# The same operations of a convolution and an attention layer in another stored order

## The chip, the core and the metric

The kernel runs on one core of a Trainium2 chip. The core has a matrix engine (TensorE, in the profile PE, its weight loads PEld), a vector engine (DVE), a scalar engine (ACT), a general engine (POOL) and a queue engine (SP), each with its own instruction stream, and 16 DMA engines. The metric is the time of one execution in device microseconds, compared by the median of several runs.

## The reference

Two independent layers share the output, 640 columns each, over 2048 tokens, in bfloat16. Layer A is a gated long convolution, layer B attention in 4 segments of 512 tokens with a memory carried from segment to segment (32 heads of 20).

```
# A: short filter of 4 taps, gate, long convolution over the sequence by FFT, gate
k_shift = sum over t of k_pad[:, t:t+S] * shift_k[:, 3-t]
kv = k_shift * v
y = irfft(rfft(kv, 2S) * rfft(ssm_k, 2S))[:S] + kv * ssm_D
a = q * y
# B: for each segment s
p = softmax(qs @ ks.T * scale + mask)      # mask: key may not come after the query
a_dot = p @ vs
a_mem = (phi(qs) @ M) / (phi(qs) @ z + 1e-6)
o = g * a_mem + (1 - g) * a_dot            # g = sigmoid(beta) per head
M = M + phi(ks).T @ vs;  z = z + sum(phi(ks))
b = o @ wo
out = concatenate([a, b])
```

## The kernel before

The kernel is not written in the order in which it runs. A recorder (class Recorder, line 105) takes down every operation with its operands and what it depends on; a group of matmuls that accumulate together is one operation. There are 1501 operations and 470 groups of PSUM banks (8 banks of 512 columns). A stored list, ORDER (line 775), then gives the sequence in which they are issued, and a second one, BASE (line 797), the first bank of each group. Both are packed numbers; unpack (line 804) makes lists of them, and Recorder.issue (line 244) goes through them:

```
for i in order:
    o = self.ops[i]
    assert all(p in seen for p in o.pred)
    for eng, method, args, kw, grp in o.calls:
        f = getattr(getattr(self.real, eng), method)
        f(*[fix(a) for a in args], ...)
```

So all instructions carry one line in the profile, L253, and are told apart by tiles. Each engine runs its own operations in the order of the list; a wait at the head of its stream holds all that stands behind it. That includes DMAs: nearly all loads and all transposes by DMA are issued from SP, one after the other, the stores to the output from POOL.

The operations have names (their keys), used below:

Layer A runs over 5 blocks of 128 channels (conv, line 378). "sk" loads the long filter (and copies it), "lk", "lv", "lq" load k, v, q; "ks" is the short filter on PE, gated into tile vt by DVE; "FK" and "FX" are the forward transforms of filter and signal on PE (Wf, 256 columns a matmul), evicted by ACT into the one tile F; "BK" and "BX" are the butterflies on DVE, "P1" to "P3" the product, "YB" the butterflies back; "I" is the inverse transform on PE, gated by DVE into outa, "O" with a block's number its store.

Layer B runs over 8 units u, two halves of 16 heads for each segment (project, line 569; attend, line 637). "P u t" projects k or q for 128 tokens (5 matmuls of 320 columns, evicted by ACT into the one tile KQ), "V u t" the values; "KT" transposes KQ by DMA into KQT, of which there are two, one for each half; "phi", "PT" and "mem" serve the memory. "bound u" finds a bound of each row's scores on DVE (tile kam, from KQT) and PE, ACT evicts it (bT), and the four copies "rows u" put it into KQT as an extra row. Then come the scores: "S u g A", "D" and "J" fill two pairs of PSUM banks with 32-row matmuls (A below the diagonal, D on it, J joined for two head groups), and two exponentials on ACT write one of 7 tiles ET, 128 x 1024 each. "O u g q" multiplies them with the values (matmuls of 21 columns), "N u g" normalises on DVE into o_s. "oT" transposes o_s, "W" projects it, "OB" stores (project_out, line 729). For the last segment "oT" and "W" come in three parts, "first", "mid" and the rest, and the accumulation in PSUM goes through all three.

In the old list, ahead of what the change moves, PE has for unit 4 the fills "S 4 3 A", "S 4 3 D" and "S 4 2 D" in a row with nothing between, the last of them the last reader of KQT before unit 6 overwrites it. At the end PE has both column halves of "W 3 3 first", then "O 7 3", then the middle parts of "oT 3".

Of the kernel before, what the change touches and what calls it, by code (L numbers as in the profile page):

```python
# [774 lines left out]
ORDER = r"""
c-jrrgLW7S5Cy>9yLan0we8flZKt+v+qP{dwQbwBZR@>nm~$qrq!5vG5?#_uJc%qRC6#25jFMUcC9_PI88TBKCNU8~;z~pb5S6b&2``x>jpUL@5?>NX42dbRB(@}!#FA7JNiwM<NhG<XMHO+0h1`-&
(jkjfm8=p?vP%LaL=MR*$&mtCkQLeRT`Ef=e3QgThB%TEv5^XCP)G_(5h*GKq@a|N(vnB=N(m_`#iY38ll)Rf%1U}<KxU*yAmShilA^Z6M;$3AHKmqRlOU-saS;z0kqI@Vu{4o}(pnlxC@C)$rGnI#
Hqu<`$~<W)4Wy~mlk8|Ap(Tv8k^&fjoM<LJkpsEV3%PL<c~B5-rJW2!d+8vZWE_U0qm0K0OhZ0&k<OAAQ6#F2L{}+<Q5cJ<7=*#-jXvlm6EF-DF&(2Z2K_Mwvt_R2M_H6dIdqr8=pnN(1HEJjW@0G5
qc7^A9~!`I5<=Nz{6G;D!v}oC94U%V_>2e^(duKCL^m_qLM%d0`H3I$3;z(#!dnzuEK6ke|Af7zugt*$%*8@kB&ARqWw2D1$$VKL^AT3mqFNsrD#N6oR6s>6MkTD2Xf_Y9^%BEY$p%?28)b!Tl7?uE
{!$zz@l!U-02wHQqy}oD7HXpoN+71Kl}4zHDu`uOQ4LKHgu1AXb+Sd8Vz@Lzh^&zjvRZ<rIliDR+MzvKpcVe2CB9*Z43@3Z0Y@dQZIkWN5u>CvcF0aSD7z%G?Unr!PTF9kbjBe$ES<1Vy5P8U#cnwu  # L780
-OwF><d+<gV{%eX$ZzR^J#t#A>sOqTB{(Bz<(x#a0Q-$UI4>9El7zM}wg&6a(pp(3>uj+tuB}BE>uPbVkzJI=*3Oz+Z|h@&t%3ElB$m`#STAd618lrZka!l~5?gyqXvwUDtwu*1XrpC}jFSX5S*Az`
f^iUsa9OU%dL**3vH?`rNixWW*kNphsOkz#lT}!Wzw%Fp8nm`9#WI-I)8sbHuF7&um20vCJFyG9F;Vs)j7HF~8c}b^b-5`~HJXOfy$G$hB%I!s=o(&QXk?9~QM8T*XkFch$8rFhuo+vh72EJcj$l6;
>QOY(V>pGTdKzc39p`WyZLPmGvpaGgXK(@CteM`Ei?}O~<RtpqLpgyAmeG3HWn95kTtj#3XRR%hwXy4HVwZ3O59GeY)LUq32{o3cwRD!=5^Hizp^3D<p0NhnSd-{&G|`vxN?yxOeIs!+jV9ID8du|K
GQESlNMR{$q&<~q@?2g>DtnA4c!)=MinN+iQ)y}q)O0%BnrnK^Y+3Cd?&AUC>j=wY88oB*vrL*<v+5`tZDVb`J+&<Q%!FfXoTauj)=~qlmA26D_QN`AC;e*QEHrCsHp^}~ET`qQT-ILmS$^xFd-RRH
wU3tDYG^Ipss*f|6|th0#|qg;`6OTDt-O<BmQ4#=cKsl2wVig>E}B4#TMjK@IrTN(;In+P+?q@CXjko~`Lv|9);9XtUfFB=W4raQm9=tK-ty}+yq6bviMM!%=Xh+Ttc;bmC-w>xtb$dxDpu91S&&sU
r}3RtvYJNLvf5V1s#{&FVfE~#g<^fnt6@0NK3G^zvI6?s!n2@8WCRw{!usCYuq~h43!7roY^qgZRerI#Hs6|Zo+-g*Y{&L&&K8_ywYW>?*iWm?aGY*+INN60UM-^g^p{0qHO{cbw!|h|ab0T5te6(n
07heEF1HmHg>@OkMqFSG`5q;-q%N}38kGyJjF#2zy53gVY74dy+hCh)jjgouT29y6M%!$MwTJf99d<;kXeq6#TdbG%)}6M?`sh{*((Sg*_Ui%d#%g*{cUw(1<{{l@`|W@ow7z=CqI0P3wLNy!y6~8_
W&<|iaa(7H?Su`}&K#^m^rQ{cL3+ea*+?CwUD=(dtrO2$3=Y>G9HFCijP}>DI!*`ZHjT&ljLDX4#ql~pdvT&xXAMr$$vQ>ru|E5-1NSolPwR2*&Fy+ZPwFYn&NEs;r|D6xs8e;i&d?k@t2x<EXX-4S
t#fsb9@F!7!Om+(UeL>WMX%X)J7?$gqFu7fcE#rDRl8w*8JqnWhjDp>H`$Z@dDCuLWxdAh9KetK#DpBgL`=;4+@TNnlmod`Z`&QaYxnHFC1Fxl(qz1-cNvTKcuAk|8B;MelQShB*h70{?-|H6Ov`jk
!4F)fulSmInUDFIff<>J3p6vcFg@pMR=(g%F4D!iL>KCJUe#+_fCX8I*Y$?p(!wmtBFx1+ys7uKxaVeBmScH7)(R}f;(VyzSb`P#KufX|pXeif%o6^NPxY?e(`<aMFSIo8=rb+prTn$N(L#QQh5ajQ  # L790
`E%Cx;Vi>S9Kj#_$&sw$w^-F*>MQ-lKfKM~9Lw<>$K|?0SLsR}%)cDPe>AWBf5k)iR!4I=#o_PtgO1@^U8mDHoijL-Ls{N8=xv?F6<o<-Ea$WNUO(!3oxn+4t)CgJA^J%x_(Xo;WKLlNujEr%**EGY
{j5v4S-0q1F6BJV=K?O|GS1;5e$lV`P1oou26HtFctH<g4PV2xe8aa~$Fg42H*ym<a|^d}F}HC8ziVh;&oExyf9MYG<SrKTu)dpn7|tX3cJAd*-N$-f+RJ!-Kfv%F*$=XzH}YTVAfk9wZ|X%nq6c^#
uj`S#sMAAvV}Hm;tmZ-Pp2U-S6F<VE{H+x|nn(8-9@AraGmq`byt%jX*51-nd7!8ExE{~r`yWl<Ej*zo_mm#T6Zv0F>?e7O$9aP3J%wlT%$~)wdN$AQIXr`B^faE<5AiU&`acz<^PHZ`b9)}o>-jvt
clS2l&5zL#3ZVhC^>#keNBL;K%qzS|#c5t*d+*@k5FQcG(K~r(@8UhYr$<CoL_>7MKyUBkeZ8Oe_W?f8m-`qGgO%RP2l-$h;zNCy5BC*5!pHhJAMa;4!6*7zUgad8?B}@5&oeBhcqB~q=|00}`YfOA
0hr@+eV$+T>psor`vPC+i+r)K@m0Rg*ZUG*>#O~gAN9z%;lUo_SNyau^@D!MkNFng>YIGCpYtd<?-#huxBCX)=!gBdpYS7o#xM9uzv;L9s_*cNzSH;kHNWj={gUtXeZI?g`+h&*{{i6J>gE
"""
# [76 lines left out]
```

## Time and profile before

| | us |
|---|---|
| median of 3 runs | 290.04 (289.86 to 291.36) |
| the profiled execution | 290.99 |
| its span, first to last instruction | 289.2 |
| PE, DVE, ACT busy | 258.5, 262.0, 254.0 |
| mean granted clock of TensorE | 0.987 |

The profiled execution took 290.99 us, of which 289.2 lie between its first and last instruction. The views used below are the page, the busy time of each engine by stretch, the waits (the engine that waited, and for whom: total, times, longest), the chain of waits that ended last, and the timeline: start and length in us, engine, operation, output tile <- input tiles, shape, count, and in brackets the idle time before it with what ended it. SPq is a DMA issue on SP; its length is that of the issue, not of the transfer.

### The profile page before, as it was taken

What the parts mean: (1) busy time and instruction counts of PE and PEld (TensorE: products, weight loads), DVE (VectorE), ACT (ScalarE), POOL (GpSimd) and SP (SyncE); (2) the same over time, 40 slices, a digit from 0 to 9 for tenths busy, and PEclk for the clock granted to TensorE, in tenths of its full rate; (3) what the DMA queues carried; (4) which work ended last, traced back from release to release, by engine and by line L of the source; (5) the groups of instructions that cost most, each with busy time, mean ns of one, the idle gap of its engine ahead of it and who ended that gap; (6) DMA issues with size and microseconds to landing.
All of it is one profiled execution on the core that took longest, in us unless ns stands there. A gap on an engine that the chain in (4) does not pass through costs nothing. (4 is left out here: it accounts for less than half of the span.)

```text
span 289.2 us, 9883 instructions
## 1 busy us (share of the span) xinstructions
PE 258.5 (89%) x4226; PEld 195.3 (68%) x4226; DVE 262.0 (91%) x398; ACT 254.0 (88%) x391; POOL 42.5 (15%) x71
## 2 busy tenths in 40 slices
PE   0999998789989899999989999998799977888895
PEld 0788756668667678777656888656586755656673
DVE  0569999999999999999999999999999999989554
ACT  1694899899998978999999999999979999989972
POOL 8300000001005000403100310022001220001620
PEclk9999999999999989999999999999799999999999
DMA  6999889899943779916696149952492029921252
GB/s 190 383 243 178 217 160 174 207 215 164 223 118 85 165 99 204 205 61 120 166 167 144 43 59 174 191 133 71 88 156 57 24 55 141 207 26 48 58 123 91
DMA packets 113500, 40.71 MB, mean 141 GB/s; under 512 B 105696, under 2 KB 111376, under 8 KB 113328
## 3 DMA queue, kind: packets, MB, share of 16 engines
q1 hardware_dynamic: 108624, 34.07, 61.8%
q0 software_dynamic: 2064, 4.76, 5.5%
q10 hardware_dynamic: 2768, 1.24, 1.8%
q8 instruction: 33, 0.54, 0.8%
q14 instruction: 11, 0.09, 0.1%
HBM read 14.11 MB, written 5.24 MB: 67 GB/s over the span
## 5 line engine op out<-in xcount | busy, mean ns | idle before, releaser
L253 ACT ACTIVATE ET<-ps 128x1024 bf16<-128x1024 f32 x160 | 155.9, 1064 | 6.7 <-PE ps L253 6.4
L253 PEld LDWEIGHTS <-xT 128*128 128x128 bf16 x640 | 60.5, 99 | 32.2 <-issue 10.8
L253 PE MATMUL ps<-wqkv,xT 128*128 128x320 bf16 x480 | 75.5, 303 | 3.6 <-ACT ET L253 1.9
L253 ACT CAST F<-ps 128x512 bf16<-128x512 f32 x80 | 43.0, 614 | 4.2 <-DVE F L253 1.6
L253 POOL DMA_DIRECT2D out_dram<-outa x32 | 22.2, 815 | 165.1 <-DVE outa L253 141.1
L253 PEld LDWEIGHTS <-ET 128*128 128x128 bf16 x1296 | 40.3, 97 | 4.1 <-issue 2.2
L253 PE MATMUL ps<-Va,ET 128*128 128x21 bf16 x1280 | 41.2, 172 | 0.1
L253 PE MATMUL ps<-KQT 32*128 32x128 bf16 (+2 forms) x896 | 34.5, 242 | 2.0 <-ACT ET L253 1.0
L253 PEld LDWEIGHTS <-Wf 128*128 128x128 bf16 x320 | 29.9, 98 | 6.5 <-issue 2.4
L253 ACT CAST KQ<-ps 128x320 bf16<-128x320 f32 x64 | 27.5, 454 | 3.7 <-PE ps L253 3.1
L253 PE MATMUL ps<-wo,xT 128*128 128x320 bf16 x160 | 25.2, 299 | 1.1 <-ACT ET L253 0.6
L253 PEld LDWEIGHTS <-KQT 32*128 32x128 bf16 x896 | 16.5, 94 | 12.0 <-issue 10.8
L253 PE MATMUL ps<-skd,kr 128*128 128x128 bf16 (+3 forms) x140 | 20.9, 301 | 1.1 <-ACT ET L253 1.0
L253 PE MATMUL ps<-Y,Wi 128*128 128x256 bf16 x160 | 20.3, 273 | 1.7 <-ACT ET L253 1.0
L253 PE MATMUL ps<-vt,Wf 128*128 128x256 bf16 x160 | 20.1, 272 | 1.8 <-DVE vt L253 1.4
L253 PE MATMUL ps<-kT,Wf 128*128 128x256 bf16 x160 | 21.2, 276 | 0.0
L253 PEld LDWEIGHTS <-kr 128*128 128x128 bf16 x140 | 17.3, 146 | 5.5 <-issue 2.7
L253 DVE TENSOR_TENSOR o<-ps,rr 128x640 bf16<-128x640 f32 x24 | 19.7, 823 | 0.7
L253 PE MATMUL ps<-mright,mleft 32*128 32x128 bf16 x512 | 14.4, 219 | 6.5 <-ACT ET L253 3.4
L253 PE MATMUL ps<-Mbd,PqT 128*128 128x84 bf16 x96 | 18.2, 202 | 1.9 <-ACT ET L253 0.9
L253 DVE TENSOR_TENSOR Y<-Y,pq 128x2048 bf16<-128x2048 bf16 (+1 forms) x20 | 18.6, 949 | 0.1
L253 DVE TENSOR_TENSOR pq<-Xh,Kh 128x2048 bf16<-128x2048 bf16 x15 | 18.3, 1223 | 0.4
(77 smaller groups left out, 356.4 us busy)
## 6 DMA issues: line engine op xcount, KB each, us to landing
vt<-in_A_v_dram SPq DMA_DIRECT2D x10, 256.0 KB
pq<-in_A_q_dram SPq DMA_DIRECT2D x10, 256.0 KB
out_dram<-outa POOLq DMA_DIRECT2D x32, 64.0 KB, 2.5
out_dram<-outb POOLq DMA_DIRECT2D x12, 160.0 KB, 3.1
ET<-in_A_ssm_k_dram SPq DMA_DIRECT2D x3, 512.0 KB
Wf<-c_wf SPq DMA_DIRECT2D x2, 512.0 KB
...
```

The costliest lines, as they stand in the source:

```text
L253: f(*[fix(a) for a in args], **{k: fix(v) for k, v in kw.items()})
```

## The change

The lists ORDER and BASE are replaced, nothing else. By its own description the new list comes from a search that charged every stretch in which PE streams few columns. All 1501 operations are the same, on the same engines, with the same shapes. On PE 309 of 502 operations stand in another place, on DVE 265 of 398, on ACT 285 of 395, on SP 90 of 139, on POOL 54 of 67; none moves by more than 25 places in its engine's order. From about the 357th operation of ACT and the 413th of PE on, up to PE's 466th, the two lists agree but for which half of a pair comes first.

```diff
 ORDER = r"""
-c-jrrgLW7S5Cy>9yLan0we8flZKt+v+qP{dwQbwBZR@>nm~$qrq!5vG5?#_uJc%qRC6#25jFMUcC9_PI88TBKCNU8~;z~pb5S6b&2``x>jpUL@5?>NX42dbRB(@}!#FA7JNiwM<NhG<XMHO+0h1`-&
...
+c-jrsgJKv85Cp)x+r7F?Z9BDX+o^5awr$%<ZQHhO+j?()VxmeMNh{GsB%P#}6p~U>Nd}21sU?<Vlt>aNnPs}nlo=8rF(jryVp;^rB_=BI<f~9BNqEU2aV3)^kTjB55?FkxA}$FfktCBOQdMGEZpkUx
...
 BASE = r"""
-c-l=<0TRO?2#W~v{~r%R?7UtrB7_jE0XXn_vsQ;8%HCM?M0v7&S^L>p#c!S+o}I@7Ms@D4r;$)Gp@^V8p00sf7crc9MwDS=s?|&yHF(x6yH0Ws?gry9BUw2WW3-N#Z}ONm#jmTSSOx2Vh{m<m06m~(
...
+c-l=<0S?3<2rCHq{~u3FCCkOB2&DzC;8*|xhJC(yR-F@$b)Qr4^`7qi?s+0y=VvL#<@w#a6SGnF!Hu&&kIkDg62u2Hn(iP9n8lbih`5D+StRdEXs(!~h8$jvUb0~_^f?)C#7b#szW2q%)0rE;RpbG(
...
```

Three places, as the instructions stand. First PE in unit 4, before the change, where the fill "S 4 3 D" ends (KQT) and "S 4 2 D" begins (mleft):

```order
5517 L253 LDWEIGHTS KQT_81
5518 L253 MATMUL ps<-KQT_81 128x128
5519 L253 LDWEIGHTS KQT_81
5520 L253 MATMUL ps<-KQT_81 128x128
5521 L253 LDWEIGHTS mleft
5522 L253 MATMUL ps<-mright,mleft 128x4x32
```

The same place after the change, from the last matmul of the group that was put in:

```order
5529 L253 LDWEIGHTS xT_94
5530 L253 MATMUL ps<-wqkv,xT_94 128x320
5531 L253 LDWEIGHTS Wf
5532 L253 MATMUL ps<-kT_103,Wf 128x256
5533 L253 LDWEIGHTS Wf
5534 L253 MATMUL ps<-kT_103,Wf 128x256
5535 L253 LDWEIGHTS Wf
5536 L253 MATMUL ps<-kT_103,Wf 128x256
5537 L253 LDWEIGHTS Wf
5538 L253 MATMUL ps<-kT_103,Wf 128x256
5539 L253 LDWEIGHTS mleft
5540 L253 MATMUL ps<-mright,mleft 128x4x32
```

A projection "P 7 1" (five matmuls of 320 columns, rows 5521 to 5530) and a transform "A 4 FK 1" (four of 256) now stand between the two fills. One of the two "P 6 0", which stood far ahead of "S 4 3 A", now stands directly behind it.

SP at the same time, before: the four transposes into KQT for unit 6, two of the memory's (PqT), and the four "rows" copies (bT).

```order
66 L253 DMA pq_110<-in_A_q_dram 128x8x128 x2
67 L253 DMA_TRANSPOSE KQT_81<-KQ 128x8x128 x4
68 L253 DMA_TRANSPOSE PqT_83<-PP 128x8x128 x2
69 L253 DMA KQT_81<-bT_119 4x512 x4
70 L253 DMA_TRANSPOSE KQT_82<-KQ 128x8x128 x4
```

And after:

```order
69 L253 DMA pq_110<-in_A_q_dram 128x8x128
70 L253 DMA_TRANSPOSE KQT_81<-KQ 128x8x128 x4
71 L253 DMA_TRANSPOSE PqT_83<-PP 128x8x128
72 L253 DMA KQT_81<-bT_119 4x512 x4
73 L253 DMA_TRANSPOSE PqT_83<-PP 128x8x128
74 L253 DMA_TRANSPOSE KQT_82<-KQ 128x8x128 x4
```

The second "PqT" moved behind the four "rows" copies.

Last PE near the end, behind "O 7 3", before:

```order
8369 L253 LDWEIGHTS o_s_122
8370 L253 MATMUL ps<-ident,o_s_122 128x128
8371 L253 LDWEIGHTS o_s_122
8372 L253 MATMUL ps<-ident,o_s_122 128x128
8373 L253 LDWEIGHTS o_s_122
8374 L253 MATMUL ps<-ident,o_s_122 128x128
8375 L253 LDWEIGHTS xT_94
8376 L253 MATMUL ps<-wo,xT_94 128x320
```

And after:

```order
8369 L253 LDWEIGHTS o_s_122
8370 L253 MATMUL ps<-ident,o_s_122 128x128
8371 L253 LDWEIGHTS o_s_122
8372 L253 MATMUL ps<-ident,o_s_122 128x128
8373 L253 LDWEIGHTS xT_94
8374 L253 MATMUL ps<-wo,xT_94 128x320
8375 L253 LDWEIGHTS xT_94
8376 L253 MATMUL ps<-wo,xT_94 128x320
```

The third middle part of "oT 3" moved behind partial sums of "W 3". The six partial matmuls ahead of "O 7 3", which read the same tiles in both lists (wo, xT_94), are those of "W 3 3" twice before, and of "W 3 1" and then "W 3 3" after. SP transposes the first parts of "oT 3" for these in the order 1, 3, 2, 0 before, and 2, 1, 3, 0 after.

More of the change, by code (lines that the diff above doesn't have):

```diff
@@ L775 @@
 ORDER = r"""
[L776 to L795, printed above, removed]
+c-jrsgJKv85Cp)x+r7F?Z9BDX+o^5awr$%<ZQHhO+j?()VxmeMNh{GsB%P#}6p~U>Nd}21sU?<Vlt>aNnPs}nlo=8rF(jryVp;^rB_=BI<f~9BNqEU2aV3)^kTjB55?FkxA}$FfktCBOQdMGEZpkUx
@@ new lines @@
+B)cS+gqBp&S~^Q^DXg+&k*t!^vRGEjW{E7ZrLx%eO=3$LD<p;GyOfgBQcQ|V9?2^uq@)y(f>K0^N<PUiWh9Q3mGo9lGFURpY)LG>CAEx}$!bb%sU?vmn$(f%QbR&XH3^c?GEd4&1qmZ@Ewu$&JZmX+
+rJmH622xQPOLJ)@Eu?@ok?fY!T1y+rVFj(JG?SawP#Q^FX(xrOgS3}U(oqUqPwQpFZG`2r+&0d}TOP}A6KtYQu>m&HM%h4{YSXNXbe7&W*813J8)JiPhz+&8)>XR6V2dKtt%wz~NjBN~T2Tv!@F;8L
+t(-+bMD(}r^2z#{BNU?JgMG9f^3#Ud4Et=q?7Pjfd{)nX*i36+3$4D*wqCNxdJ6E*h&eV}mP&7#E6ZfDm9oCFSeD3qnInP)QpQT#LWzP|Qo$-&Mf)L(q>s$A`4(0bD`l0em!UFD`pE{_C{fX02FMcI
+Bn@q#43frH+*V5o3zi!8Qx;fFt7Ro^tu(S|h=Ju|m}|AIj;)Z&R>i7XH4CzJGDNCd6KiTAGF(Q;C>bfutga1~&9X(-$X3}V&8?-iwRYCt_DU=JYb|Vtw6X2d!467m+a>$ufb5ixwom@Z9yu*x5gCW1
@@ new lines @@
+lO2~c5)<F-q@0jb(%HUP7wc-V(9OErQTb}eWVig1!_oyu<gA>N-_{ksrHA#zAM1rR7EadMI%|Z+=#7?$gjVQ-b_k6y2tWfgL?^^XTy#bp#6x^skn?g$s%v6gl=fI{A(jBamIO&5+8iw~03DDFssk}u
+rbr@mL~=}(K}d*$cGwQt5R8`zGD#-NXc;4yWt?1*6}HOO8+DqvZm^BE(oCU$<(~}3Qrls*b*GJ$UAEh<$~D<z;dHr$(FnTCHraIvul4kX?6t6ZQ*KLC9g2t=O+#sDjjk~?vPRN68bt$ipB=FMR#!LM
+7Tapu?3Ns{Cvwyp>M7f9$Lz5*)kb>O&e<8eBhB=#9JjV;h92mT^LE-USYo|s_vF5`#tA!V59N_$Kqg$aD|Xec*>%f^q}m4E&;;Gl6n$~Y`r(G%vIi1V)8Y)$BbKJaQ+X!O<+cq&GEJz7w7xdbB>GZb
+$!mEdu{Dmy)#MsaQy_(=LOM-}#=29}>qs=w;dpFMEVTye3rV2&?7rQxyY|3RYAQ{mY4xE!vZpoznUNL$kOfa6{Ei<Oh0z#~XGo0<no$FhNi*wLWYPHAT+<*l+iD9PgLYa|YiKRqsx7sZ=0!eyLpF>>
@@ L801 @@
+F@zYGY&q&e@6F_4`Y*E!qj~oK1H$S_!f!%iI^og`O?HjfR?ndxZL06CU!@;s7zTO
 """
```

16 lines of the change are left out of this document (13 added, 3 removed).

## The prediction

> **What bounds the kernel now.** I read the page first, then the busy times of three stretches, the waits of each engine, the chain of waits, and last the timeline at the places that the new order touches. From the page, and from the view of busy time by stretch (per stretch: length, then PE, PEld, DVE, ACT, POOL, granted clock, DMA share, GB/s):
>
> ```profile
> span 289.2 us, 9883 instructions
> ...
> PE 258.5 (89%) x4226; PEld 195.3 (68%) x4226; DVE 262.0 (91%) x398; ACT 254.0 (88%) x391; POOL 42.5 (15%) x71
> ...
> 0.00:30.00 30.00, 22.68 (x186) 18.54 (x187) 17.17 (x28) 16.93 (x35) 8.17 (x19) 1.00 0.98 252
> 30.00:250.00 220.00, 203.66 (x3327) 152.05 (x3325) 217.32 (x318) 206.53 (x319) 26.60 (x40) 0.98 0.72 136
> 250.00:289.20 39.20, 32.13 (x722) 24.68 (x718) 27.55 (x54) 30.54 (x39) 7.77 (x12) 0.99 0.37 80
> ```
>
> Three engines look equally full on the page; the stretches separate them. From 30 to 250 us DVE is busy 217.32 of 220.00 us, ACT only 206.53, PE 203.66. Who waits, asked for that stretch alone (DVE, then the two largest of ACT):
>
> ```profile
> DVE outa L253 <- issue: 0.2, 1, 0.2
> ...
> ACT ET L253 <- PE ps L253: 5.0, 10, 1.0
> ACT KQ L253 <- PE ps L253: 2.5, 7, 0.8
> ```
>
> DVE has one wait of 0.2 us in 220 us; ACT waits for PE 7.5 us in these two rows alone, and DVE does not feel it. So the middle is DVE's, and no order of the same DVE instructions can make it shorter than about its busy time: 220.00 - 217.32 = 2.7 us is all there is, much of it seams between instructions. Behind it stands the tail:
>
> ```profile
> 250.07 0.29 DVE L253 TENSOR_TENSOR A<-sel,kam 128x128 bf16<-128x128 bf16 x1
> ...
> 258.65 0.36 DVE L253 RECIPROCAL rr<-ps 128x32 f32<-128x32 f32 x1 [1.03 <-PE ps L253]
> ...
> 206.20 10.80 PE ps L253 x178
> ...
> 217.02 0.03 ACT ET L253
> ...
> 277.63 8.42 PE ps L253 x136
> 286.05 0.02 issue
> 286.07 0.43 ACT kT L253
> ```
>
> The first row is the last step of "bound 7", the second the first wait of DVE in the tail (1.03 us), the rest are pieces of the chain that ended last: PE for 10.80 us from 206.20, ACT's exponentials from 217 on, PE from 277.63 to 286.05, one eviction, the store. From "bound 7" on, PE and ACT have the same set of groups ahead and behind in both orders. So the new time is the time at which "bound 7" and its neighbours are reached, plus the same tail, plus what changes inside the last few groups.
>
> **The change part by part.** No instruction is added or removed; only places and banks move.
>
> *The clock.* The stretches in which the granted clock fell:
>
> ```profile
> 100.00:101.00 1.00, 0.54 (x2) 0.33 (x3) 1.00 (x2) 1.00 (x2) 0.00 (x0) 0.80 1.26 278
> 101.00:102.00 1.00, 1.00 (x6) 0.67 (x4) 1.00 (x2) 1.00 (x2) 0.00 (x0) 0.50 0.47 90
> ...
> 104.00:105.00 1.00, 1.00 (x22) 0.88 (x24) 0.88 (x2) 1.00 (x2) 0.00 (x0) 1.00 1.21 246
> 206.00:207.00 1.00, 0.80 (x32) 0.63 (x31) 1.00 (x3) 1.00 (x2) 0.00 (x0) 0.70 0.00 0
> 207.00:208.00 1.00, 1.00 (x9) 0.73 (x6) 1.00 (x3) 1.00 (x2) 0.00 (x0) 0.50 0.06 16
> ...
> 209.00:210.00 1.00, 1.00 (x26) 0.89 (x25) 0.97 (x2) 1.00 (x2) 0.00 (x0) 0.59 0.62 133
> 210.00:211.00 1.00, 1.00 (x32) 0.95 (x29) 1.00 (x1) 0.18 (x1) 0.00 (x0) 1.00 0.54 109
> ```
>
> A clock of 0.80 in a microsecond means half speed for its last 0.4 us, so the first dip is 100.6 to 104.0, and by 0.70 and 0.59 the second is 206.4 to 209.8: 3.4 us each, 1.7 us of PE work lost each. DVE (third figure) stays at 1.00 through both; ACT pays later (0.18 at 210). What reaches DVE is at most the 0.88 at 104 (0.1 us) and the 0.2 us wait above. Both dips avoided is worth 0.2 to 0.3 us in the middle; I take **-0.2**. The dips begin 206.4 - 100.6 = 105.8 us apart, 31 times 3.41 us. [...]
>
> *The score fill of unit 4.* The new order takes a projection group (5 matmuls of 320 columns) and a filter transform (4 of 256) ahead of the last fill "S 4 2 D". The fills before, and the price of such groups at full clock:
>
> ```profile
> 203.53 0.40 PE L253 MATMUL ps<-KQT 32*128 32x384 bf16 x8
> 204.11 0.23 PE L253 MATMUL ps<-mright,mleft 32*128 32x128 bf16 x2 [0.18 <-ACT KQ L253]
> 205.04 0.40 PE L253 MATMUL ps<-mright,mleft 32*128 32x128 bf16 x14 [0.70 <-ACT ET L253]
> ...
> 206.20 0.47 PE L253 MATMUL ps<-mright,mleft 32*128 32x128 bf16 x16 [0.54 <-DVE o L253]
> 206.42 0.68 PE L253 MATMUL ps<-KQT 32*128 32x128 bf16 x16
> ...
> 214.65 0.60 PE L253 MATMUL ps<-kT,Wf 128*128 128x256 bf16 x4
> 215.09 1.52 PE L253 MATMUL ps<-wqkv,xT 128*128 128x320 bf16 x10
> ```
>
> Five of 320 are 0.76 us (half of 1.52), four of 256 are 0.44 (215.09 - 214.65): 1.20 us together. PE idled 0.18 + 0.70 + 0.54 = 1.42 us here, so between none and all of the 1.20 us shows at the fill. What is queued behind it: SP's four transposes of KQ, which overwrite KQT and so wait for this fill, and DVE's "bound 6", which reads them:
>
> ```profile
> 206.95 6.32 SPq L253 DMA_TRANSPOSE KQT<-KQ  x4
> ...
> 217.24 2.28 DVE L253 TENSOR_REDUCE kam<-KQT 128x4 f32<-128x2048 bf16 x1
> ...
> 33.70 1.82 SPq L253 DMA_DIRECT2D KQT<-bT  x3
> ...
> 37.82 0.12 PEld L253 LDWEIGHTS <-KQT 32*128 32x128 bf16 x8 [0.26 <-issue]
> ```
>
> The issue ends at 213.27, the reader starts at 217.24: 3.97 us of margin. A copy's data is usable about 37.82 - 35.52 = 2.3 us after its issue ends (the last two rows, where PE stood for it). So "bound 6" has 1.67 us to spare. All of the 1.20 us fits in it: cost 0, at most 0.3 if the transposes land later than the copy; I take **+0.1**. The second transpose type stays on SP: the first "PqT" still follows them, the second goes behind the four "rows" copies, which its reader in unit 6, more than 20 us later, does not notice.
>
> *The last groups.* Before "O 7 3" PE now runs the first partial of "W 3 1" and then of "W 3 3", where it ran two of "W 3 3"; SP's order of the four transposes for them is 2, 1, 3, 0 instead of 1, 3, 2, 0:
>
> ```profile
> 273.14 6.18 SPq L253 DMA_TRANSPOSE xT<-o_s  x4
> ...
> 278.81 0.99 PE L253 MATMUL ps<-wo,xT 128*128 128x320 bf16 x6
> 279.64 0.20 PE L253 MATMUL ps<-Mbd,PqT 128*128 128x84 bf16 x1
> ```
>
> PE used to need the second transpose (issued by 273.14 + 3.09 = 276.23) at 278.81 and did not wait, so it lands in less than 2.58 us. Now it needs the third (issued by 277.78) after 3 matmuls, at 279.26. With 2.3 us it comes at 280.1, 0.8 us late, with 2.58 at 280.4, 1.1 late; with 1.5 or less it is free. Behind it in PE's queue stands "O 7 3" itself, and nothing covers that: 0 to 1.1 us on the chain, I take **+0.5**, since the data of one transpose is short work. After that PE has the same 20 "W" and 4 "oT" matmuls between the last o_s and the end in both orders: 0.
>
> *Everywhere else.* Two hundred and sixty-five of DVE's 398 places change. Before, the 7.5 us that ACT waited cost DVE 0.2 at most. A like order makes like waits; DVE starts from none, so it can only gain some: from 0 to about 1, the size of one of ACT's longest waits (1.0) passed on whole. I take **+0.4**.
>
> The head stays: the first 30 us hold the same groups in nearly the same order, and "ident" is issued one place earlier, the last x tile no earlier. W 2 0's eviction (0.48 us) goes ahead of the end of "bound 7" on DVE; its rows are in place long before ACT comes to unit 7: 0.
>
> Sum: -0.2 + 0.1 + 0.5 + 0.4 = **+0.8 us**. On the profiled execution (290.99 us, a span of 289.2 and 1.79 around it) that is 291.8; it lay 0.95 above the median of the runs, so the forecast is 290.04 + 0.8 = **290.8 us**. A measurement of this kernel tells 0.5%, 1.45 us, from no change.
>
> **The rivals.**
> *Slower: the scores of unit 4 come late.* If PE does not swallow the two groups and idles again for the same three reasons, the fill comes 1.20 + 1.42 = 2.6 us later. From 1.67 us on, "bound 6" waits, on the engine that has no spare time, and the exponentials of that fill and the value groups behind it are 2.6 us late too, so DVE's "N 4" steps wait as well. For it: PE's 10.80 us behind this place in the chain, the single KQ buffer, the one KQT buffer of this half. Against: PE's 1.42 us of idle, and DVE's record of not feeling ACT. Time: 290.04 + 2.6 = 292.6; a second such place passes on as much.
> *Faster: the waits go.* DVE's small gaps shrink (0.2 and perhaps 0.8 of the 2.7 us), and the 1.03 us wait at 258.65 goes as ACT is on time: 290.04 - 2.0 = 288.0. For it: ACT is 13.5 us short of full in the middle (220.00 - 206.53). Against: DVE has to deliver as before, and nearly every gap of it would have to close.
> *The clock's whole price is on the path.* 2 dips x 1.7 = 3.4 us off: 286.6. Against it stands DVE's 1.00 in both dips.
> *The change doesn't do what it says.* A dip falls elsewhere. DVE then pays 0.1 to 0.3 us, as in the two seen: 291.0, inside the forecast.
>
> **How the numbers follow.** No change that can be told 0.47 (with a dip elsewhere 0.15 of it), its own range 289.3 to 291.5, that is -0.7 to the bound of 1.45; slower, by unit 4 or a place like it, 0.38; faster by the waits 0.12, by the clock 0.03. The range must reach into both: 288.2, where the faster case lies, to 293.2, unit 4's 2.6 us and 0.6 of the tail; some 0.17 is left out. Faster 0.15, same 0.47, slower 0.38.
>
> **What would show it.** DVE's waits from 30 to 250 us: under 1 us by the forecast, 2 or more if the slower case holds, with "kam<-KQT" among the waiters. PE's first "wo" group before the last value group with a DMA wait of about half a microsecond. The granted clock: if 1.00 everywhere and the time still about 290, the clock was not on the path. Wrong would be a span under 287.5 with DVE still busy 217 of 220 us, for then the middle was not DVE's.

## The result, and the profile after

The changed kernel took 290.26 us (288.68 to 291.22, median of 20 runs), the kernel before 291.26 us on the same chip (20 runs): a ratio of 0.996 with a 95% interval of 0.9944 to 0.9975. It is about 1.0 us faster, and the interval excludes no change. The forecast was 0.8 us slower, with "no change that can be told" as the likeliest case. That 290.26 lies close to the forecast 290.8 is chance: the forecast started from a median of three runs, 290.04, and the same kernel gave 291.26 in these twenty. Below, every kernel is compared with before on its own chip.

The profiled execution of after is the fastest of its twenty (288.68 us). Its page, and its busy time by stretch (length, PE, PEld, DVE, ACT, POOL, granted clock, DMA share, GB/s):

```profile
span 286.9 us, 9859 instructions
...
PE 258.9 (90%) x4226; PEld 193.2 (67%) x4226; DVE 261.3 (91%) x398; ACT 253.3 (88%) x391; POOL 42.3 (15%) x71
...
0.00:30.00 30.00, 23.14 (x201) 18.69 (x202) 17.80 (x28) 16.75 (x35) 8.08 (x19) 1.00 0.97 249
30.00:250.00 220.00, 205.30 (x3357) 151.34 (x3355) 217.91 (x323) 207.74 (x321) 26.50 (x40) 1.00 0.73 139
250.00:286.90 36.90, 30.43 (x674) 23.18 (x671) 25.58 (x49) 28.86 (x37) 7.72 (x12) 1.00 0.31 74
```

The granted clock is 1.00 in all three stretches, where before had 0.98 and 0.99. DVE is busy 217.91 of 220.00 us in the middle, as full as before with 217.32. Yet the same work is done sooner. The timeline of DVE gives the first and the last step that mark the middle, the end of "bound 0" and the end of "bound 7", in before (its last step stands in the prediction, at 250.07) and then in after:

```profile
31.91 0.29 DVE L253 TENSOR_TENSOR A<-sel,kam 128x128 bf16<-128x128 bf16 x1
```

```profile
31.35 0.28 DVE L253 TENSOR_TENSOR A<-sel,kam 128x128 bf16<-128x128 bf16 x1
...
248.26 0.28 DVE L253 TENSOR_TENSOR A<-sel,kam 128x128 bf16<-128x128 bf16 x1
```

From one to the other it is 218.16 us before and 216.91 after, though after also has the 0.48 us eviction of "W 2 0" inside. DVE's waits between 30 and 250 us, with the two largest of ACT, are as few as before:

```profile
ACT ET L253 <- PE ps L253: 3.9, 11, 0.7
ACT KQ L253 <- PE ps L253: 2.6, 8, 0.9
...
DVE Kh L253 <- ACT F L253: 0.2, 1, 0.2
```

So a middle that was "DVE's" before and is DVE's after lost 1.25 us, and no wait tells where. The busy time between the two steps isn't fixed either (stretch and its length, DVE's busy time and rows, granted clock, DMA share, GB/s; before, then after):

```profile
32.20:250.36 218.16, 215.48 (x317) 0.98 0.72 134
```

```profile
31.63:248.54 216.91, 214.85 (x319) 1.00 0.72 137
```

It is 0.63 us less after, with one instruction more inside, and the idle time is 2.06 us instead of 2.68. The end of the chain of waits shows a loss on the other side, the transposes for "W 3" with PE behind them:

```profile
266.29 4.42 PE ps L253 x136
270.70 0.74 SPq L253
271.49 1.25 SPq L253
272.78 3.91 DMA xT<-o_s
276.74 6.69 PE ps L253 x88
283.52 0.49 DVE kT L253
```

### The profile page after: what moved, and what is told of

It reads as the page before. It is cut to its first block, busy times and chain, and to the rows that moved or that the text cites. A ratio compares the mean times of both kernels' runs of the same rounds, so it can differ in the third digit from the quotient of the medians.

```text
span 286.9 us, 9859 instructions
## 1 busy us (share of the span) xinstructions
PE 258.9 (90%) x4226; PEld 193.2 (67%) x4226; DVE 261.3 (91%) x398; ACT 253.3 (88%) x391; POOL 42.3 (15%) x71
## 4 chain that ended last, share of the span: by engine, by line
DVE 36%; PE 30%; ACT 15%; issue 6%; SPq 6%; DMA 5%; ACTq 0%; DVEq 0%
PE ps L253 30%; ACT ET L253 12%; DVE Y L253 9%; SPq L253 6%; DVE Xh L253 5%; DVE pq L253 3%; DVE kam L253 3%; DVE o L253 3%; DMA wqkv<-in_B_wq_dram 3%; ACT F L253 3%; DVE Kh L253 2%; DVE outa L253 2%; DVE qabs L253 2%; DMA xT<-o_s 1%; DVE F L253 1%
## 5 line engine op out<-in xcount | busy, mean ns | idle before, releaser
L253 PEld LDWEIGHTS <-xT 128*128 128x128 bf16 x640 | 59.7, 98 | 29.9 <-issue 8.3
L253 PE MATMUL ps<-wqkv,xT 128*128 128x320 bf16 x480 | 74.4, 301 | 1.8 <-ACT ET L253 1.2
L253 ACT CAST F<-ps 128x512 bf16<-128x512 f32 x80 | 44.1, 634 | 4.0 <-DVE F L253 1.8
L253 PE MATMUL ps<-KQT 32*128 32x128 bf16 (+2 forms) x896 | 35.9, 239 | 4.1 <-ACT ET L253 1.6
L253 ACT CAST KQ<-ps 128x320 bf16<-128x320 f32 x64 | 28.1, 478 | 3.4 <-PE ps L253 3.1
L253 PEld LDWEIGHTS <-KQT 32*128 32x128 bf16 x896 | 17.4, 92 | 15.5 <-issue 14.4
L253 PE MATMUL ps<-vt,Wf 128*128 128x256 bf16 x160 | 20.8, 272 | 1.1 <-DVE vt L253 0.7
L253 PE MATMUL ps<-skd,kr 128*128 128x128 bf16 (+3 forms) x140 | 20.2, 291 | 0.6 <-ACT ET L253 0.5
L253 DVE TENSOR_REDUCE kam<-KQT 128x4 f32<-128x2048 bf16 x8 | 18.2, 2277 | 0.0
```

Of the source, the lines that this page charges most:

```text
L253: f(*[fix(a) for a in args], **{k: fix(v) for k, v in kw.items()})
```

## The experiments

Kernels e1 to e6, e9, e14 and e15 mix the two stored orders: the order of before up to some place of the list, then that of after, or the other way. An operation that stands on both sides of a cut is issued in the first part that has it, and the few that a cut leaves out (three in e2, e9 and e15, one in e3 and e6) at the first cut. Kernel e0 is before again, e8 and e16 are after again, and the others move or repeat single operations. One table first. "Dips" counts the 3.4 us stretches at half clock in the profiled execution. "Middle" runs from the end of "bound 0" to the end of "bound 7" on DVE; an asterisk marks kernels with the eviction of "W 2 0" inside. "ACT" is the time from the end of unit 7's bT to the exponential of "S 6 2 D" on ACT, and "tail" that from the end of ACT's "S 7 3 D" to the last "W 3 0".

| kernel | median / before (us) | ratio, 95% | dips | middle | ACT | tail |
|---|---|---|---|---|---|---|
| before, first profile | | | 2 | 218.16 | 3.27 | 6.97 |
| after, first profile | 290.26 / 291.26 | 0.996, 0.9944 to 0.9975 | 0 | 216.91* | 1.95 | 7.36 |
| e0 before | 291.42 / 291.26 | 1.0003, 0.9979 to 1.0028 | 2 | 218.35 | 3.22 | 6.98 |
| e1 head | 291.54 / 291.26 | 1.0010, 0.9991 to 1.0028 | 0 | 217.49 | 2.99 | 7.25 |
| e2 early | 290.14 / 291.25 | 0.9965, 0.9939 to 0.9992 | 1 | 218.08 | 3.37 | 6.94 |
| e6 unit 4 | 290.31 / 291.25 | 0.9979, 0.9951 to 1.0006 | 0 | 217.62 | 1.97 | 6.94 |
| e3 late | 290.39 / 291.26 | 0.9954, 0.9931 to 0.9978 | 1 | 217.16* | 2.81 | 7.06 |
| e4 tail | 290.78 / 291.26 | 0.9987, 0.9961 to 1.0014 | 1 | 218.22 | 3.19 | 7.42 |
| e8 after | 290.33 / 291.25 | 0.9968, 0.9947 to 0.9989 | 0 | 216.95* | 1.95 | 7.49 |
| e16 after | 290.30 / 291.06 | 0.9968, 0.9944 to 0.9993 | 1 | 216.88* | 3.14 | 7.31 |
| e5 without tail | 289.61 / 291.25 | 0.9938, 0.9912 to 0.9964 | 0 | 216.91* | 1.97 | 6.93 |
| e14 without tail | 290.22 / 291.06 | 0.9961, 0.9934 to 0.9989 | 0 | 216.96* | 3.13 | 6.96 |
| e9 middle alone | 289.59 / 290.57 | 0.9957, 0.9937 to 0.9977 | 0 | 217.01* | 1.97 | 6.95 |
| e15 middle alone | 289.52 / 291.06 | 0.9939, 0.9910 to 0.9968 | 0 | 216.89* | 1.97 | 6.97 |
| e13 one swap | 290.14 / 291.06 | 0.9963, 0.9935 to 0.9991 | 0 | 216.90* | 2.97 | 6.94 |
| e10 repeats, before | 290.69 / 290.57 | 0.9988, 0.9965 to 1.0011 | 1 | 217.52 | 3.18 | 7.74 |
| e11 repeats, after | 290.66 / 290.57 | 1.0014, 0.9988 to 1.0041 | 0 | 217.23* | 2.95 | 7.24 |
| e12 PT late, before | 290.69 / 291.37 | 0.9991, 0.9963 to 1.0020 | 0 | 217.74 | 1.97 | 6.98 |
| e17 apart | 288.46 / 291.45 | 0.9881, 0.9849 to 0.9912 | 0 | 216.16* | 1.97 | 6.94 |
| e18 apart, before | 291.09 / 291.45 | 0.9993, 0.9964 to 1.0022 | 2 | 218.45 | 1.97 | 6.95 |

### The change in pieces

Before again, and the new order in one piece of the list at a time, the rest as before:

```diff
 e0  order = before
-order = before
+e1  order = after[:145] + before[145:]                        # head
+e2  order = before[:143] + after[143:866] + before[866:]      # early
+e6  order = before[:866] + after[866:1142] + before[1142:]    # unit 4
+e3  order = before[:866] + after[866:1318] + before[1318:]    # late
+e4  order = before[:1318] + after[1318:]                      # tail
```

> The kernel before once more, unchanged, for a second profile and for the granted clock of every execution beside its time. Theory ORDER (the gain is that ACT's exponentials and PE reach the last units earlier, and DVE has no wait there): the same 1 us wait of DVE at the first normalising step 'N 6 2' of the tail is there again, DVE is busy 217 of 220 us in the middle again, and executions at clock 1.0 are less than 0.5 us faster than those at 0.98 to 0.99. Rival CLOCK (the gain is the dips avoided): executions at clock 1.0 are 1 to 3.4 us faster than those at 0.987. Rival CHANCE (the profiled execution after the change was merely a fast one): milestones such as the end of 'bound 7' on DVE (250.36 before, 248.54 after) differ between two profiles of this same kernel by 1 to 2 us.

> The new order for the first 145 operations alone (to about 32 us), the old one behind. DVE's idle time of the first 30 us was 12.82 us before and 12.21 after the change. If the head is part of the gain: 0.4 to 0.6 us faster, 'bound 0' 0.5 us earlier, the 1 us wait at 'N 6 2' still there. Rival CLOCK and the forecast (the head stays): within 0.3 us of before.

> The new order for operations 143 to 866 alone (30 to 165 us), where the first dip of the profile of before lies. DIPS: it avoids about half of the dips (0.5 an execution instead of 1.0), worth 0.3 us; DVE's way from 'bound 0' to 'bound 7' 217.5 to 217.9 us against 218.2 before; the late signal at 'S 6 2 D' stays. Rival ORDER (DVE's gaps shrink in the early units): 0.6 us or more faster. Forecast (a like order makes like waits, plus 0.4): 0.2 to 0.6 us slower.

> The new order for operations 866 to 1142 alone (165 to 219 us: unit 4 with the two groups ahead of 'S 4 2 D', and the second dip). DIPS: never two dips, 0.3 to 0.6 us faster than before. Forecast (the fill a little late, +0.1, dip -0.1): no change. Rival of the forecast (unit 4 late): 0.4 to 2.6 us slower, with DVE waiting at 'bound 6'. If the whole gain of the new order for 866 to 1318 (0.9 us) comes from here: 0.7 to 1.0 us faster.

> The new order for operations 866 to 1318 alone (units 4 and 5 and the way to 'bound 7', 165 to 250 us), the old one ahead and behind. Theory ORDER: the larger part of the gain, 0.6 to 1.3 us faster, and DVE's 1.03 us wait at 'N 6 2' gone although the order around 'N 6 2' is the old one, since ACT comes to it earlier. Rival of the forecast (units 4 late): 0.4 to 2.6 us slower, with DVE waiting at 'bound 6'. Rival CLOCK: faster by at most the second dip, 1.7 us, and only in executions at clock 1.0 against those with the dip. Rival CHANCE: within 0.3 us.

> The new order for the operations behind 'bound 7' alone (from the 1318th, 250 us on), the old one ahead. By the forecast's term for the last groups: 0.3 to 0.6 us slower, PE waiting 0.2 to 1.1 us for the third transpose of o_s ahead of 'O 7 3', and the 1.03 us wait at 'N 6 2' still there. If instead the order behind 'bound 7' is what removes the wait at 'N 6 2': 0.5 us or more faster, with that wait gone. Rival CLOCK: within 0.3 us.

The head alone is worth nothing that can be told. The early and the late piece each take 0.9 to 1.1 us off the medians; the piece around unit 4 as much, with an interval that just holds 1. The tail's interval holds 1 too, but its profile has what the forecast named, PE waiting for a transpose, and the longest tail of the six. The early and the late piece (which contains that around unit 4) would add up to 2.0 us, where the two together, e9 and e15 below, give 1.0 and 1.5. With intervals of some 0.7 us to each side that can be chance; or part of the gain is something that either piece can bring alone. The clock is one such thing.

**The clock.** Each execution lists its granted clock. Of 177 executions of before in these runs, 50 had none of the dips (clock 0.998 or more) with a mean of 290.42 us, 84 had one (0.992 to 0.994) with 291.27, and 43 had two (0.986 to 0.988) with 291.69. A line with one slope for all, and a level of its own for each chip, gives 0.62 us a dip, with a standard error of 0.09; an execution of before has 0.96 dips on average. Of the 44 executions of after in the first comparison, e8 and e16, 26 had none (290.13 us), 18 had one (290.36; two at 0.997 are counted here) and none had two: 0.41 an execution. The mean of all is 291.13 for before and 290.22 for after, 0.91 apart. Without any dip the two are 290.42 - 290.13 = 0.29 apart, with a standard error of 0.18; the dips add 0.71 us to the mean execution of before and 0.09 to that of after, and the difference of these, 0.62, is the clock's part.

The order has a say in where a dip falls. In the profiles they begin at 100.4 to 101.1 us (before, e0, e4, e18) or 205.2 to 206.9 (before, e0, e2, e10, e18), all where the list is that of before, and no profile with the new order at these places has one there. Those of e16 and e3 begin at 250.4 and 252.2 us, behind "bound 7", so dips are rarer with the new order and not gone. Whether a dip comes at a place differs between executions of one order, which have none, one or two. In the clock record of before's trace both dips last 3.413 us at a clock of 0.50, and the second begins 105.813 us behind the first, 31 times that length; what sets the moment is not shown. The prediction's -0.2 takes both dips of its one profile as avoided; over all executions the new order has fewer of them and not none, 0.41 an execution against 0.96.

Where a dip costs is not where it is seen. Two pairs of neighbours on DVE in the timeline, first in before, with its two dips, then in e1, which has the same order there and no dip:

```profile
103.38 1.22 DVE L253 TENSOR_TENSOR Y<-Y,Xh 128x2048 bf16<-128x2048 bf16 x1
104.72 0.69 DVE L253 TENSOR_TENSOR vt<-ps,vt 128x512 bf16<-128x512 f32 x1
...
220.03 0.28 DVE L253 TENSOR_TENSOR A<-sel,kam 128x128 bf16<-128x128 bf16 x1
220.48 0.69 DVE L253 TENSOR_TENSOR outa<-ps,pq 128x512 bf16<-128x512 f32 x1 [0.16 <-issue]
```

```profile
104.14 1.21 DVE L253 TENSOR_TENSOR Y<-Y,Xh 128x2048 bf16<-128x2048 bf16 x1
105.27 0.68 DVE L253 TENSOR_TENSOR vt<-ps,vt 128x512 bf16<-128x512 f32 x1
...
220.36 0.28 DVE L253 TENSOR_TENSOR A<-sel,kam 128x128 bf16<-128x128 bf16 x1
220.56 0.68 DVE L253 TENSOR_TENSOR outa<-ps,pq 128x512 bf16<-128x512 f32 x1
```

From start to start it is 1.34 against 1.13 us, and 0.45 against 0.20: 0.21 and 0.25 lost on readers of PSUM, the second one 10.7 us behind the end of its dip at 209.8. Only 0.16 of it has the form of a wait. Laid row by row beside e1, the profiles with the old order on DVE keep pace to some hundredths of a microsecond, but for a few steps. The first dip is followed by 0.20 and 0.13 us at 104.7 and 115.0 us in before, by the same two within 0.01 us in e0 and e4, and in these two by 0.26 and 0.28 more at 128. The second is followed by 0.25 at 220.5 in before and 0.17 in e0; e4, without it, has nothing there. In e10, whose only dip begins at 205.2, all steps together are 0.03 us. So a dip costs the middle 0.03 to 0.6 us. (Not every such step is a dip's: e12, which has none, loses 0.25 us at 181.6, at the reader of a transposed KQT.)

### The change again, and without its ends

```diff
-order = after
+e8, e16  order = after
+e5, e14  order = after[:1318] + before[1318:]                 # old tail
+e9, e15  order = before[:143] + after[143:1318] + before[1318:]   # old head and tail
```

> The changed kernel once more, for a second profile and more executions with their clocks; its first profile was the fastest of its 20 runs. Theory DIPS (an avoided dip is worth about 0.6 us each, 0.8 dips an execution fewer, and the rest of the gain is there at equal clock): clock 1.0 in some three of four executions, their mean 0.3 to 0.6 us under the executions of before at 1.0. Theory LATE SIGNAL (in five profiles with the old order somewhere, ACT stood 0.8 to 1.36 us at 'S 6 2 D' although the fill had ended, because PE's signal came late; in the first profile after the change it didn't): this wait is absent again, and 'S 5 3 D' to 'S 6 3 D' on ACT takes 18.8 us instead of 19.6. Rival CHANCE: the wait is there as in the others, and this profile is 1 us longer than the first.

> The changed kernel a third time, on the same chip as the three others: 0.8 to 1.2 us faster than before, clock 1.0 in most executions, no wait of ACT over 0.3 us at 'S 6 2 D', PE waiting 0.2 us or more for a transpose of o_s ahead of 'O 7 3'.

> The new order up to 'bound 7', the old one behind it: the change without its tail. By the forecast's term for the last groups (the third transpose late, 0.3 to 0.5 us in the profiles of the change and of its tail alone): 0.3 to 0.6 us faster than the change itself, so 1.3 to 1.7 under before, and no DMA wait of PE ahead of 'O 7 3'. If the order behind 'bound 7' is what removes the wait of ACT at 'S 6 2 D': that wait is back, and it is 0.5 to 1 us slower than the change.

> The change without its tail once more, beside the change on one chip: 0.4 to 0.7 us faster than the change if the tail's loss is real; by CHANCE within 0.2 us.

> The new order for operations 143 to 1318 alone: the change without its head and without its tail. Theory PARTS (middle faster, tail 0.4 to 0.7 us slower, head not faster): 289.2 to 289.7 us where before gives 291.25, at least as fast as the change without its tail (289.61), and 0.6 to 1.1 us faster than the change. Rival CHANCE (parts within 0.3 us of nothing): 290.3 or more. The wait of ACT at 'S 6 2 D' is absent, as in every kernel so far with the new order in unit 4.

> The change without its head and tail once more, on the same chip: as the change without its tail within 0.3 us (the head is worth nothing), 0.4 to 0.7 us faster than the change. If the new head costs something: 0.3 us or more faster than the change without its tail.

After is 0.9968 both times. In the seven profiles of this group and of the first comparison the middle takes 216.88 to 217.01 us (the one dip, in e16, lies behind it). The old order without a dip takes 217.49 and 217.74 (e1, e12), and with the new order around unit 4 alone 217.62 (e6). That gain of 0.7 is there every time, and e3 has it with the late piece alone (217.16, eviction inside).

In this group the last part is 6.93 to 6.97 us long with the old tail, with the new one 7.31 to 7.49: the new tail costs 0.45. The old tail isn't always free of the wait, though. PE stands 0.15 us for the second transpose in e1 and 0.65 in e10, where the tail is 7.25 and 7.74:

```profile
279.33 0.99 PE L256 MATMUL ps<-wo,xT 128*128 128x320 bf16 x6 [0.65 <-DMA xT<-o_s]
```

The head makes no difference that can be told (e9 and e15 against e5 and e14). Ratios with the old tail run from 0.9938 to 0.9961, so the tail's loss is about the size of the spread between repeats: on one chip e15 is 0.78 us under e16, but e14 only 0.08. The lengths in the profiles show the loss better than the medians, for "bound 0" itself ends anywhere from 31.30 us (e9) to 34.01 (e5).

### One swap in the tail

In the new list, one column half of "W 3 3 first" and one of "W 3 1 first" trade places, with their banks exchanged, so that PE has both halves of the same group ahead of "O 7 3" again:

```diff
-W 3 1 first, W 3 3 first, O 7 3, oT 3 2 mid, oT 3 1 mid, W 3 2 first, W 3 1 first
+W 3 1 first, W 3 1 first, O 7 3, oT 3 2 mid, oT 3 1 mid, W 3 2 first, W 3 3 first
```

> The changed kernel with two partial sums on PE exchanged: ahead of 'O 7 3' it now runs both column halves of 'W 3 1' (these need the second transpose of o_s only), and the first of 'W 3 3' (which needs the third) comes where the second of 'W 3 1' was; the two banks are exchanged with them. If the forecast's term for the last groups is right in kind (PE stands for the third transpose in front of 'O 7 3'): the DMA wait there is gone, the way of ACT from 'S 7 3 D' to the last 'W 3 0' is 7.0 us as before instead of 7.4 to 7.5, and the kernel is 0.3 to 0.6 us faster than the change. Rival (the loss in the tail comes from other moves there): under 0.15 us.

PE at the first "wo" groups, in the timeline, of after and then of e13:

```profile
275.93 0.57 PE L253 MATMUL ps<-wo,xT 128*128 128x320 bf16 x3
276.74 0.58 PE L253 MATMUL ps<-wo,xT 128*128 128x320 bf16 x3 [0.25 <-DMA xT<-o_s]
277.16 0.20 PE L253 MATMUL ps<-Mbd,PqT 128*128 128x84 bf16 x1
```

```profile
276.71 0.98 PE L253 MATMUL ps<-wo,xT 128*128 128x320 bf16 x6
277.53 0.20 PE L253 MATMUL ps<-Mbd,PqT 128*128 128x84 bf16 x1
```

After takes 277.16 - 275.93 = 1.23 us to the next group, e13 0.82, in one piece with no wait for a DMA. The tail is 6.94 us again. The term of the tail is shown in the profiles, place and size; the medians (290.14 against 290.30 of e16 on the same chip) don't show the 0.3 to 0.6 us that were expected.

### A late signal from PE

In before, ACT waits 1.35 us for the fill "S 6 2 D", and DVE 1.03 us behind it. In after neither waits here. ACT's timeline from the bT of unit 7 on, two exponentials and then that of "S 6 2 D", in before and in after:

```profile
251.39 0.59 ACT L253 CAST bT<-ps 128x512 bf16<-128x512 f32 x1
251.95 1.94 ACT L253 ACTIVATE ET<-ps 128x1024 bf16<-128x1024 f32 x2
255.25 3.77 ACT L253 ACTIVATE ET<-ps 128x1024 bf16<-128x1024 f32 x4 [1.35 <-PE ps L253]
```

```profile
249.46 0.59 ACT L253 CAST bT<-ps 128x512 bf16<-128x512 f32 x1
250.11 3.83 ACT L253 ACTIVATE ET<-ps 128x1024 bf16<-128x1024 f32 x4
254.21 4.69 ACT L253 ACTIVATE ET<-ps 128x1024 bf16<-128x1024 f32 x5 [0.27 <-PE ps L253]
```

The wait of 0.27 us in the last row is for a later fill. And PE at the end of the fill, in before and in after:

```profile
253.50 0.39 PE L253 MATMUL ps<-KQT 32*128 32x128 bf16 x16
253.94 1.52 PE L253 MATMUL ps<-wo,xT 128*128 128x320 bf16 x10
```

```profile
251.57 0.39 PE L253 MATMUL ps<-KQT 32*128 32x128 bf16 x16
252.10 1.52 PE L253 MATMUL ps<-wo,xT 128*128 128x320 bf16 x10
```

After's fill ends at 251.97, and its exponential, the third of four without a break, starts at 252.00. Before's ends at 253.89 us by its rows, and ACT, free since then, starts at 255.25, 1.36 us later; in the trace's semaphore events PE's signal comes at 255.22. Late signals came with the time at which the copies "rows 7" land: in every late profile the release lies 0.03 to 0.14 us behind the first of them. Two explanations were tried. CROSSING: the signal is late where the fill and ACT's exponential ahead of it end within some hundredths of a microsecond of each other, as in before (253.89 both); the first matmul of the fill, repeated, makes the fill some 0.3 us longer (0.95 us in e10 against 0.63 in before), more than the 0.1 expected. HELD: SP's second "PqT" transpose ahead of the four copies holds them, and the signal with them; it goes behind the copies.

```diff
-for eng, method, args, kw, grp in o.calls:
+calls = o.calls
+if o.eng == "PE" and tuple(o.key) == ("S", 6, 2, "D"):
+    calls = [o.calls[0]] * 6 + list(o.calls)      # e10, on before; * 5 in e11, on after
+for eng, method, args, kw, grp in calls:
```

```diff
  L253 DMACopy pq_110<-in_A_q_dram 128x8x128 x2
+ L253 DMACopy KQT_82<-bT_119 4x512 x4
  L253 DmaTransposeAnt PqT_84<-PP 128x8x128
- L253 DMACopy KQT_82<-bT_119 4x512 x4
```

> The order of before, with the first matmul of the fill 'S 6 2 D' given seven times instead of once (it writes the same values again), some 0.1 us more of TensorE, so that the fill ends about 0.1 us behind ACT's exponential before it and not with it. Theory CROSSING (the late signal at 'S 6 2 D' comes of the hundredths of a microsecond by which the fill and that exponential end together): ACT's wait there falls from 1.0 to 1.4 us to about 0.2, 'S 5 3 D' to 'S 6 3 D' on ACT takes 18.7 to 18.9 us instead of 19.6, and the kernel is up to 1 us faster though it has more work. Rival (the signal is late because of something else going on then, such as the four 'rows' copies that land at 255): the wait stays at 1.0 to 1.4 us, and the time does not change.

> The changed kernel, with the first matmul of 'S 6 2 D' given six times instead of once, some 0.07 us more, so that the fill ends where ACT's exponential before it ends. Theory CROSSING: ACT now waits 0.8 to 1.3 us at 'S 6 2 D', which it did not in two profiles of the change, and the kernel is 0.5 to 1 us slower than the change. Rival: the wait stays under 0.2 us, no change of time.

> The order of before with one issue on SP moved: the second PqT transpose for unit 7 goes behind the four 'rows 7' copies instead of ahead of them; PE, DVE and ACT keep their orders. In ten of eleven profiles PE's signals that came late near 'S 6 2 D' came within 0.15 us of the first landing of 'rows 7', and those copies stood behind this transpose, whose packets were held for 1.2 to 1.9 us. Theory HELD (what holds the transpose and the copies behind it also holds PE's signal): ACT's wait at 'S 6 2 D' is gone or under 0.3 us, DVE's wait at 'N 6 2' too, and the kernel is 0.5 to 1 us faster than before. Rival (the moment at which the fill ends decides alone): the wait stays at 1.0 to 1.4 us, no change of time.

ACT's waits for PE between 248 and 262 us, in e10, in e11 and in e12 (the kernels with repeats have three lines more, so their line is L256; the wait of e12 is for a later fill):

```profile
ACT ET L256 <- PE ps L256: 1.3, 1, 1.3
```

```profile
ACT ET L256 <- PE ps L256: 0.9, 1, 0.9
```

```profile
ACT ET L253 <- PE ps L253: 0.2, 1, 0.2
```

The repeats make after late, as CROSSING says, but don't make before timely, against it. Moving the transpose makes before timely, as HELD says; but e6 was timely with the transpose where before has it. And the column "ACT" has e13, e14 and e16 late with the order of after at this place. So neither holds as it was put, and the cause stays open.

The traces hold one sign that joins the two. In every profile but e12, packets of SP's second "PqT" transpose take 1.3 to 1.9 us. Where the fill ends within 0.74 us of the start of the first such packet, the signal is on time (five profiles); where it ends 0.96 us or more behind it, the signal is late (eight); between 0.77 and 0.89 us three are late and three on time; e12, without such packets, is on time. One reading, which no run was made for and which is not shown, is that a signal that falls due late in such a stretch comes only at its end.

What is known is the price: with the same order, e14 reaches the end of "W 3 0" 252.89 us behind "bound 0" and e5 252.01; e16, late and with a dip there, 253.33, and after and e8, on time, 252.39 and 252.68. So it is some 0.6 to 0.9 us when it happens. The kernel with this alone, e12, cannot be told from before (0.9991).

### Neighbours on DVE that depend on each other

If the middle is shorter with the same instructions and equal waits, the rows must follow each other more closely. Over the 316 rows of DVE between the two "bound" steps, a row that by the recorder's dependences needs the row directly ahead of it starts 0.04 us behind that row's end, and one that doesn't starts 0.08 us ahead of it (the expectations below have 0.07), so a dependent neighbour costs 0.12 us more. The old order has 58 such dependent neighbours, the new one 52, and e3 has 53. From old to new that is 6 x 0.12 = 0.7 us. The test takes the order of e9 and moves nine instructions of DVE by one place so that 41 are left; e18 does the same with six moves to the old order, 58 to 50. One of the nine:

```diff
  L253 TensorTensor Kh_106<-F_105 128x4x512
- L253 TensorTensor F_105<-F_105 128x2048
  L253 TensorTensor o_s_121<-ps,rr_124 128x4x80
+ L253 TensorTensor F_105<-F_105 128x2048
  L253 TensorReduce kam_115<-KQT_81 128x4
```

> The change without head and tail, with nine DVE instructions between 70 and 225 us each put one place earlier, between two neighbours of which the second uses what the first has just written or read. Theory PAIRS (such a neighbour starts 0.04 us behind the end of the first, an independent one 0.07 us ahead of it; the old order has 58 such pairs between 'bound 0' and 'bound 7', the new one 52): nine pairs less at 0.11 us, so 1.0 us less from the end of 'bound 0' to the end of 'bound 7' on DVE, 215.9 to 216.1 us where the unchanged version has 216.9 to 217.0 in both of its profiles. If DVE alone sets the end there, the whole is 0.5 to 1.0 us faster, ratio to before 0.991 to 0.993 against 0.9957 and 0.9939. Rival BOTH ENGINES (ACT is full from 219 to 250 us and holds the end by itself): that stretch of DVE is shorter only by what its waits for ACT and PE leave, 216.5 to 217.0, and the ratio stays at 0.994 to 0.996. By the forecast's view (DVE's busy time is the bound, and order cannot shorten it): no change.

> The order of before with six DVE instructions between 130 and 240 us put one place earlier in the same way. PAIRS: 0.66 us less from 'bound 0' to 'bound 7' on DVE than the old order has at the same number of dips (218.2 to 218.35 with two, 217.5 to 217.7 with none), and up to 0.6 us faster. Rival BOTH ENGINES and the forecast: no change over 0.2 us.

The place of that move in DVE's timeline, in e9 and then in e17:

```profile
73.63 1.23 DVE L253 TENSOR_TENSOR Kh<-F 128x2048 bf16<-128x2048 bf16 x1 [0.20 <-ACT F L253]
74.89 1.22 DVE L253 TENSOR_TENSOR F<-F 128x2048 bf16<-128x2048 bf16 x1
76.03 0.48 DVE L253 TENSOR_TENSOR o_s<-ps,rr 128x320 bf16<-128x320 f32 x1
76.43 2.28 DVE L253 TENSOR_REDUCE kam<-KQT 128x4 f32<-128x2048 bf16 x1
```

```profile
75.05 1.23 DVE L253 TENSOR_TENSOR Kh<-F 128x2048 bf16<-128x2048 bf16 x1 [0.20 <-ACT F L253]
76.19 0.48 DVE L253 TENSOR_TENSOR o_s<-ps,rr 128x320 bf16<-128x320 f32 x1
76.59 1.22 DVE L253 TENSOR_TENSOR F<-F 128x2048 bf16<-128x2048 bf16 x1
77.72 2.28 DVE L253 TENSOR_REDUCE kam<-KQT 128x4 f32<-128x2048 bf16 x1
```

The lengths are the same to 0.01 us; the step from "Kh" to the row behind it is 1.26 us with its dependent and 1.14 with another, and from "Kh" to "kam" it is 2.80 against 2.67. Nine moves bring the middle to 216.16 us, 0.73 to 0.85 under the two kernels with the same order otherwise (217.01 and 216.89), just outside the 215.9 to 216.1 expected by PAIRS and well under the rival's 216.5. Eleven dependent neighbours fewer are 11 x 0.12 = 1.3 us; gaps over 0.1 us give 0.46 of it back, 0.35 of them a wait for a transpose. The gain reaches the end: from "bound 0" to the end of the last "W 3 0" it is 251.01 us, against 251.88 in e9 and 251.78 in e15. At 0.9881 (six executions of 288.46 us by the median, against 291.45) e17 is the fastest kernel here and the only one more than 1% under before. That is 3.0 us, more than the 1.0 and 1.5 of e9 and e15 and the 0.8 of the moves together. What the rest is, and how much of it the few executions are, isn't shown.

In the old order the same cure did nothing, for DVE then comes to some readers before their data. DVE's waits from 30 to 250 us in e18:

```profile
DVE qabs L253 <- DMA KQT<-KQ: 0.6, 1, 0.6
...
DVE kam L253 <- DMA KQT<-KQ: 0.4, 1, 0.4
```

One microsecond of new waits for transposes, where 8 x 0.12 = 1.0 was to be had, and two dips in this profile: 218.45 us. PAIRS had expected 0.66 us less.

## Why the prediction was wrong

The four terms, as forecast and as the runs show them:

| term | forecast (us) | measured (us) |
|---|---|---|
| the clock | -0.2 | -0.6 |
| the score fill of unit 4 | +0.1 | 0 |
| the last groups | +0.5 | +0.45 |
| everywhere else in the middle | +0.4 | -0.7 |
| sum | +0.8 | -0.85 (means -0.91, medians -1.0) |

**The step that failed** is in the first part: "the middle is DVE's, and no order of the same DVE instructions can make it shorter than about its busy time". From it the term "everywhere else" was built: "DVE starts from none" (no waits), "so it can only gain some". The middle was DVE's, and is still, but its busy time is no fixed floor. A row counts as busy from start to end, and two rows that don't depend on each other overlap by 0.08 us while two that do leave 0.04 between them. DVE, whose rows nearly all touch, is 99% busy either way. Between the two "bound" steps it is busy 215.48 of 218.16 us in before, 215.13 in e1 without dips, 214.85 in after, and 214.02 of 216.16 in e17. With 58 dependent neighbours at 0.12 us each, some 7 us hang on the order, and none of it shows as a wait; how much of it an order can have is another matter (e18).

The prediction had the clue, "much of it seams between instructions", and took the seams as fixed. So the term came out with the wrong sign: 0.7 saved, and 1.1 like for like, since the eviction of "W 2 0" (0.48 us, some 0.4 with its overlap) now lies inside. Six fewer dependent neighbours are 0.7 of these 1.1. Larger gaps give another 0.2: gaps over 0.1 us come to 0.76 us in before, 0.48 in e1 with the clock whole, and 0.30 in after. That fewer dependent neighbours shorten the middle was put to the test and holds (e17); that they are most of what this change gained there rests on the sum above.

**The clock** was mis-sized, -0.2 for -0.6. The mechanism was right: of PE's loss of 1.7 us a dip about two thirds are absorbed, for 0.62 us a dip shows in the time. The price was read at the dip itself, from DVE's busy share and its one wait, while most of the loss (0.38 of 0.58 us in before) appears 10 us and more behind it, as wider steps that the waits hardly list. Fewer dips alone, 0.55 an execution at 0.62 us, are 0.34; more than half of the rest of the 0.6 is that the 18 executions of after with a dip lost only 0.23 us to it. Whether its dips fall where they cost less, or these are too few to tell, stays open.

**Unit 4** was right. Its two groups ahead of the fill make no wait on DVE in e6, where they stand alone, and "bound 6" is not late. The rival built on it, 292.6, fell.

**The tail** was right in place and size: the wait for the third transpose is there, and it is 0.45 us longer from the last exponentials to the last "W 3 0". That before "did not wait" for the second transpose is true of the profile that was read, but not of every one with the old tail (e1, e10).

**The rival that came nearest** is "the waits go" (288.0). Its sign and its engine were right. Of its 2.0 us, 1.1 came from DVE's gaps and seams; the 1.03 us wait at 258.65 goes in some executions and not in others, for the late signal is not bound to this change; the tail gave 0.45 back, and the eviction of "W 2 0" 0.4. With the clock's 0.6 that makes some 0.9, as measured: inside what the forecast called no change, but on the other side of zero.

By the prediction's own marks, DVE's waits stayed under 1 us and PE waited for a transpose where it should, as forecast. The last mark, "a span under 287.5 with DVE still busy 217 of 220 us", would show the reasoning wrong; the profiled execution has 286.9 and 217.91. It is the fastest of twenty, so the span alone would prove little; the middle of 216.9 in seven profiles does. The mark's own reading, "for then the middle was not DVE's", doesn't hold: DVE waits 0.2 us there in after as in before.
